# Attention with a threshold and a gated convolution block: 28 of 128 full softmax tiles are transposed by the DMA crossbar, by way of DRAM

## The chip, the cores and the metric

The kernel runs on one core of one Trainium2 chip. The metric is the device time of one execution in microseconds (us). Three runs of the kernel before gave 926.75, 927.73 and 929.31 us; their median is 927.73 us.

## The reference

There are 8 batches of 8 heads, 576 tokens, 64 values to a head. All arrays are float32.

```python
scores = (1/8) * q @ k.T                              # per batch and head, 576 x 576
scores = where(scores >= max(scores) - tau, scores, -1e9)
attn   = exp(scores - max(scores));  attn /= sum(attn) + 1e-9
x      = attn @ v                                     # heads side by side: 576 x 512 per batch
h      = relu(x @ w_in)                               # 576 x 1024
c[t]   = cw[0]*h[t-1] + cw[1]*h[t] + cw[2]*h[t+1]     # along the tokens, per channel
out    = (h * sigmoid(c)) @ w_out                     # 576 x 512
```

## The kernel before

The tokens of a batch are cut into five row tiles: four of 128 rows and one of 64. Two heads are worked on together as a pair, so a batch has four pairs, numbered p = 0 to 3, and the whole run has 160 units of (batch, pair, tile), 128 of them with 128 rows. A batch is walked in two chunks of tiles, (0, 1) and (2, 3, 4); inside a chunk the pairs follow each other, even pairs with the tiles in rising order and odd pairs in falling order.

A unit computes the scores of 128 rows against all 576 keys of both heads (`ps_s`, lines 537 and 544), takes the row maximum on DVE (L552), the exponential on ACT (L561), the mask and row sum on DVE (L564), and scales the rows, mostly on POOL (L597). The result is the tile `em`, 128 x 1152 (two heads of 576). For the product with v it must stand with the keys on the partitions, so it is turned in nine blocks of 128 x 128. TensorE does that against an identity (`turn` and `turns`, L626), four blocks to a PSUM tile `ps_t`; ACT copies each PSUM tile to the tile `eT` of the pair (`group`, L621). `eT` has 128 partitions, nine blocks of 320 columns each, and the row tiles of a chunk lie side by side in the columns. The ninth blocks of the chunk's row tiles share one PSUM tile (`odd`), and the 64-row tile takes one group of four for both heads.

When an odd pair is done, `attend` multiplies `eT` of two pairs with v (`pa`, L676 and L685); ACT and DVE move `pa` into `x` (L692, L695). `ps_t` and `pa` share two PSUM buffers, and `eT` has two buffers. The gated block works chunk by chunk: `mm1` (`ph`, L713), the taps and the gate on DVE, ACT and POOL, and `mm2` (`po`, L786), whose result ACT copies to `ot` (L793) and SP writes out (L794).

SP issues nearly all DMAs, in one in-order queue: loads of q, k and v, the copies `q<-q`, `ks<-ks` and `ks<-xk` that lay out the two halves of a split operand (`halves`, L477), and the stores.

The order of the instructions on each engine is made ahead of time by `Plan.run`. Each step is recorded with `op(engine, ns, function, w=..., r=..., ahead=...)`: a cost in ns, the pieces that it writes and reads, and how far ahead of its place it may go. The planner plays these through, and whatever is ready with the lowest rank goes next on a free engine. Its pieces can be parts of a tile: `(eT, (off, i, k))` is one group's part of `eT`. Waits between engines are put in afterwards, from the memory that each instruction touches. An engine takes its instructions strictly in the order that the planner wrote, and one that waits holds up all behind it.

Of the kernel before, what the change touches and what calls it, by code (L numbers as in the profile page):

```python
# [10 lines left out]
F32 = mybir.dt.float32  # L11
F32R = mybir.dt.float32r
I64 = mybir.dt.int64
U32 = mybir.dt.uint32
AF = mybir.ActivationFunctionType
ALU = mybir.AluOpType
PSUM = bass.MemoryType.PSUM
# [3 lines left out]
AHEAD = {'s': 6.25, 's4': 7.75, 't': 3.5, 'a': 3.5, 'prep': 4.25, 'w': 2.5, 'load': 7.75}  # L21
# [26 lines left out]
}  # L48

JOINT = 2  # L50

KEEP = {'rows': 2.304, 'cols': 1.613, 'turn': 3.226, 'full': 2.304}

# [192 lines left out]
def tile_tau_attention_gated_ffn(  # L246
# [14 lines left out]
    nc = tc.nc  # L261
    P = 128
    B, NP, _, _, S = qd.shape
# [22 lines left out]
    cpool = ctx.enter_context(tc.tile_pool(name="cpool", bufs=1))  # L286
    wk = ctx.enter_context(tc.tile_pool(name="wk", bufs=2))
    sm = ctx.enter_context(tc.tile_pool(name="sm", bufs=4))
    ps_s = ctx.enter_context(tc.tile_pool(name="ps_s", bufs=2, space=PSUM))
    ps_t = ctx.enter_context(tc.tile_pool(name="ps_t", bufs=2, space=PSUM))  # L290
    ps_w = ctx.enter_context(tc.tile_pool(name="ps_w", bufs=2, space=PSUM))
# [23 lines left out]
    def copy(e, dst, src, scale=1.0):  # L315
        if e == "act":
            nc.scalar.activation(dst, src, AF.Copy, scale=scale)
        elif scale == 1.0:
            engines[e].tensor_copy(dst, src)
        else:  # L320
            engines[e].tensor_scalar(dst, src, scale, None, op0=ALU.mult)
# [5 lines left out]
    def sp(n):  # L327
        return 2.6 * n

    def act(n, psum=False):  # L330
        return n * 0.833 + (58 if psum else 95)

    def dve(n, fixed=65):
        return n * 1.07 + fixed
# [4 lines left out]
    def pool1(n):  # L339
        return n * 0.9 + 225  # L340
# [100 lines left out]
    def plain(b):  # L441
        return b == 0
# [73 lines left out]
    def unit(u, k, q1, q2, o, n):  # L516
# [2 lines left out]

        heads = [[0, 1]] if 2 * n <= P else [[0], [1]]  # L520
        m, rows = len(heads), n * len(heads[0])
        em = plan.buf(wk, "em", 4, [P, 2 * S], F32, f"em_{u}")

        few = plan.buf(sm, "few", 4, [P, 10], F32, f"few_{u}")
        a = AHEAD["s" if 2 * n > P else "s4"]
# [79 lines left out]
            )  # L605
        return em

    def transposes(u, ems, tiles, eT):


        em, n, off = ems[-1]

        def group(i, reads, parts, *evacs, width=4 * P):

            pt = plan.buf(ps_t, "ps_t", 2, [P, 512], F32, f"ps_t_{u}_{i}")
            op(
                "pe", width * 0.852, lambda: parts(pt), w=[(pt, 0)], r=reads + [(ident, 0)], ahead=AHEAD["t"], kind="turn"
            )
            for k, (w, dst, src) in enumerate(evacs):
                op(  # L620
                    "act", act(w, True), lambda dst=dst, src=src: nc.scalar.activation(dst(), src(pt), AF.Copy),  # L621
                    w=[(eT, (off, i, k))], r=[(pt, 0)], ahead=AHEAD["t"]
                )

        def turn(pt, at, em, b):
            nc.tensor.transpose(out=pt[:, at:at + P], in_=em[:, int(b * P):int(b * P) + P], identity=ident[:])  # L626

        def turns(pt, b0):
            for i in range(4):
                turn(pt, i * P, em, b0 + i)  # L630

        def both():
            x = eT[:, 0:4, off:off + n]
            return bass.AP(tensor=x.tensor, offset=x.offset, ap=[x.ap[0], [5 * x.ap[1][0], 2], *x.ap[1:]])

        if n < P:
            group(0, [(em, 0)], lambda pt: turns(pt, 0), (4 * P, both, lambda pt: pt[:].rearrange("p (i j n) -> p j i n", i=4, j=2)))
        else:  # L640
            for b0 in (0, 4):
                group(
                    b0, [(em, 0), (em, 1)] if b0 else [(em, 0)], lambda pt, b0=b0: turns(pt, b0),
                    (4 * P, lambda b0=b0: eT[:, b0:b0 + 4, off:off + P], lambda pt: pt[:].rearrange("p (a b) -> p a b", a=4))
                )
        if len(ems) < tiles:
            return
        full, small = ([x for x in ems if (x[1] < P) == y] for y in (False, True))
        w = len(full) * P


        def odd(pt):
            for x in full + small:
                turn(pt, x[2], x[0], 8 if x[1] == P else 3.5)

        parts = [(w, lambda: eT[:, 8, :w], lambda pt: pt[:, :w])]
        for _, m, at in small:
            for j in range(2):
                parts.append((
                    m, lambda j=j: eT[j * D:(j + 1) * D, 4, at:at + m], lambda pt, j=j: pt[D:, w + j * m:w + (j + 1) * m]  # L660
                ))
        group(8, [(x[0], 1 if x[1] == P else 0) for x in full + small], odd, *parts, width=w + len(small) * P)
# [155 lines left out]
    def order(i):  # L818
        c, p = pairs[i]
        return chunks[c].tiles[::-1] if p % 2 else chunks[c].tiles  # L820
# [36 lines left out]
    for now in range(len(units) + 1):  # L857
        plan.rank = float(now)
        if now < len(units):
            i, t = units[now]  # L860
            c, p = pairs[i]
            tiles, (o, w), (a0, an) = order(i), chunks[c].new, chunks[c].cols
            at, n = TILES[t]
            em = unit(now, *(whole[i] if n == P or i not in last else last[i]), at - o if n == P or i not in last else 0, n)
            if t == tiles[0]:
                eT = plan.buf(wk, "eT", 2, [P, NBLK, 320], F32, f"eT_{i}")
                ems = []
            ems.append((em, n, at - o))
            transposes(now, ems, len(tiles), eT)
            if t == tiles[-1]:  # L870
                x = plan.buf(wk, f"x{c % 2}", NP, [P, 2, XW[c % 2]], F32R, f"x_{i}")
                xs.setdefault(c, []).append(x)
                off = o - a0
                if off:
                    y, end = xs[c - 1][p], chunks[c - 1].cols[1]
                    op(
                        "pool", 110, lambda x=x, y=y, off=off, end=end: nc.gpsimd.tensor_copy(x[:, :, :off], y[:, :, end - off:end]),
                        w=[(x, 2)], r=[(y, 0), (y, 1)]
                    )
                waiting.append((i, p, eT, vts[i], x, off))  # L880
# [74 lines left out]
```

## Time and profile before

| | |
|---|---|
| median of three runs | 927.73 us |
| span of the profiled execution | 923.8 us |
| PE matmul busy | 896.7 us, 97% |
| DVE busy | 741.1 us, 80% |
| ACT busy | 701.2 us, 76% |
| POOL busy | 582.1 us, 63% |
| DMA queue of SP and ACT, share of the 16 DMA engines | 38.6% |
| granted TensorE clock | 0.996 |

The span runs from the first to the last instruction of the one execution that was profiled; the times of the runs hold some 4 us beside it. Busy times are sums over the span; since matmuls are pipelined and their ends are modelled, a busy PE need not be one at its peak. In the rows of the profile "x28" is the number of instructions, "<-" stands between what is written and what is read, and the time after a second "<-" is how long the engine sat idle until the named one released it. SPq is SP's issuing of DMAs.

### The profile page before, as it was taken

How to read it: one execution, taken by the hardware profiler on the slowest of the kernel's cores; microseconds unless marked ns; L12 is line 12 of the kernel's file. 1: busy time of each engine (PE TensorE's matmuls, PEld its weight loads, DVE VectorE, ACT ScalarE, POOL GpSimd, SP SyncE). 2: the span in 40 equal slices, each digit the busy share in tenths (PEclk: the TensorE clock that was granted, in tenths of full speed). 3: DMA queues.
4: the chain of work that ended last, by engine and by line, in shares of the span. 5: the costliest groups of instructions: out<-in, count | busy, mean ns of one | idle time of the engine just before them, and what ended most of it. 6: DMA issues, size and time to landing. Idle time of an engine off the chain costs nothing.

```text
span 923.8 us, 19667 instructions
## 1 busy us (share of the span) xinstructions
PE 896.7 (97%) x6308; PEld 731.8 (79%) x6308; DVE 741.1 (80%) x1853; ACT 701.2 (76%) x1590; POOL 582.1 (63%) x1028
## 2 busy tenths in 40 slices
PE   5989899999999999999999999999999999999998
PEld 2446588878889788879888787887888888887897
DVE  5988999979868798878967789886977879896643
ACT  5888898878678787869768687786958788785653
POOL 3665887767747586666746677675865757664422
PEclk9999999999999999999999999999999999999999
DMA  6643363355341652345423453416523265221000
GB/s 211 200 151 128 97 166 101 111 146 167 87 122 40 176 150 83 84 115 140 122 91 81 133 148 103 120 59 166 161 85 95 55 175 140 83 79 60 13 24 34
DMA packets 77926, 104.02 MB, mean 113 GB/s; under 512 B 18560, under 2 KB 49536, under 8 KB 77824
## 3 DMA queue, kind: packets, MB, share of 16 engines
q1 hardware_dynamic: 76960, 100.86, 38.6%
q10 hardware_dynamic: 864, 1.90, 0.6%
q8 instruction: 51, 0.84, 0.4%
q14 instruction: 51, 0.42, 0.1%
HBM read 58.88 MB, written 9.44 MB: 74 GB/s over the span
## 4 chain that ended last, share of the span: by engine, by line
PE 79%; ACT 9%; DVE 6%; issue 2%; DMA 2%; POOL 1%; SPq 0%; ACTq 0%; POOLq 0%; DVEq 0%
PE po L786 21%; PE ph L713 16%; PE ps_t L626 13%; PE pa L685 12%; PE ps_s L544 11%; PE ps_s L537 4%; ACT eT L621 2%; PE pa L676 2%; DVE em L564 2%; ACT em L561 2%; DVE few L552 1%; DVE t L748 1%; PE pw_stage L394 1%; DMA q<-in_qd_dram 1%; ACT hp L728 1%
## 5 line engine op out<-in xcount | busy, mean ns | idle before, releaser
L597 POOL TENSOR_SCALAR em<-em,few 128x576 f32<-128x576 f32 x285 | 258.3, 914 | 36.9 <-DVE few L588 27.3
L564 DVE SCALAR_TENSOR_TENSOR em<-ps_s,few,em 128x576 f32<-128x576 f32 x288 | 228.1, 812 | 51.0 <-ACT em L561 44.9
L713 PE MATMUL ph<-x,w1h 128*128 128x322 f32 (+1 forms) x1024 | 243.2, 305 | 0.7 <-ACT hp L728 0.7
L552 DVE TENSOR_REDUCE few<-ps_s 128x1 f32<-128x576 f32 x288 | 210.8, 748 | 29.4 <-PE ps_s L537 15.2
L561 ACT ACTIVATE em<-ps_s,few 128x576 f32<-128x576 f32 x288 | 206.7, 743 | 30.9 <-DVE few L552 26.0
L621 ACT ACTIVATE eT<-ps_t 128x512 f32<-128x512 f32 (+2 forms) x416 | 203.3, 512 | 16.9 <-PE ps_t L626 15.2
L626 PE MATMUL ps_t<-ident,em 128*128 128x128 f32 x1312 | 187.7, 276 | 4.6 <-DVE x L695 1.7
L626 PEld LDWEIGHTS ps_t<-ident,em 128*128 128x128 f32 x1312 | 152.3, 141 | 34.2 <-POOL em L597 11.0
L713 PEld LDWEIGHTS ph<-x,w1h 128*128 128x128 f32 x1024 | 174.9, 189 | 3.7 <-issue 1.8
L748 DVE SCALAR_TENSOR_TENSOR t<-hp,cw,t 128x255 f32<-128x255 f32 (+1 forms) x256 | 151.9, 597 | 25.9 <-ACT t L732 18.8
L544 PE MATMUL ps_s<-ks,q 128*128 128x288 f32 x896 | 155.0, 304 | 2.6 <-DVE em L564 1.6
L713 PE MATMUL ph<-x,w1l 128*128 128x322 f32 (+1 forms) x512 | 151.1, 295 | 0.0
L544 PEld LDWEIGHTS ps_s<-ks,q 128*128 128x128 f32 x896 | 129.0, 188 | 13.8 <-issue 4.6
L324 POOL TENSOR_TENSOR gl<-t,gh 128x255 fp32r<-128x255 f32 (+9 forms) x192 | 121.4, 644 | 29.4 <-ACT gh L765 29.2
L685 PE MATMUL pa<-eT,v 128*64 128x320 f32 (+1 forms) x1024 | 133.3, 412 | 0.0
L685 PEld LDWEIGHTS pa<-eT,v 128*64 128x64 f32 x1024 | 70.9, 138 | 59.9 <-issue 16.7
L786 PE MATMUL po<-w2h,gh 128*128 128x512 f32 x288 | 118.1, 410 | 0.0
L786 PE MATMUL po<-w2h,gl 128*128 128x512 f32 x288 | 113.0, 392 | 0.5 <-POOL gl L324 0.5
L786 PE MATMUL po<-w2l,gh 128*128 128x512 f32 x288 | 113.1, 393 | 0.0
L713 PEld LDWEIGHTS ph<-x,w1l 128*128 128x128 f32 x512 | 96.6, 189 | 0.1
L755 DVE SCALAR_TENSOR_TENSOR t<-t,hp 128x321 f32<-128x321 f32 (+1 forms) x128 | 70.8, 554 | 14.3 <-ACT t L757 13.6
L757 ACT ACTIVATE t<-t 128x321 f32<-128x321 f32 (+1 forms) x128 | 56.9, 445 | 24.4 <-DVE t L748 24.1
(69 smaller groups left out, 1019.6 us busy)
## 6 DMA issues: line engine op xcount, KB each, us to landing
q<-q SPq DMA_DIRECT2D x336, 64.0 KB, 2.0
v<-in_vc_dram SPq DMA_DIRECT2D x64, 288.0 KB, 3.3
k<-in_kp_dram SPq DMA_DIRECT2D x35, 320.0 KB, 3.6
out_dram<-ot SPq DMA_DIRECT2D x36, 256.0 KB, 2.0
xk<-in_kt_dram SPq DMA_DIRECT2D x28, 288.0 KB, 3.3
ks<-xk SPq DMA_DIRECT2D x56, 144.0 KB, 2.4
xq<-in_qt_dram SPq DMA_DIRECT2D x56, 128.0 KB, 2.3
stage<-in_w_out_dram SPq DMA_DIRECT2D x8, 512.0 KB, 3.5
```

Source lines behind the costliest of these rows:

```text
L324: engines[e].tensor_tensor(dst, x, y, op=ALU.subtract)
L544: nc.tensor.matmul(ps[:, c, :CH], lhsT=q[:, h, o:o + n], rhs=k[:, h, c * CH:(c + 1) * CH], start=(i == 0), stop=(i == 1))
L552: nc.vector.tensor_reduce(few[:rows, nm], ps[:rows, :, :CH], op=ALU.max, axis=mybir.AxisListType.XY, negate=True)
L561: nc.scalar.activation(view(), ps[:rows, :, :CH], AF.Exp, bias=few[:rows, nm])
L564: nc.vector.scalar_tensor_tensor(view(), ps[:rows, :, :CH], few[:rows, th], view(), op0=ALU.is_ge, op1=ALU.mult, accum_out=few[:rows, total])
L597: engines[e].tensor_scalar(sl, sl, by, to, op0=ALU.mult, op1=ALU.add)
L621: "act", act(w, True), lambda dst=dst, src=src: nc.scalar.activation(dst(), src(pt), AF.Copy),
L626: nc.tensor.transpose(out=pt[:, at:at + P], in_=em[:, int(b * P):int(b * P) + P], identity=ident[:])
L685: nc.tensor.matmul(pa[j * D:(j + 1) * D, :w], lhsT=vt[:, blk, :], rhs=eT[:, blk, :w], start=False, stop=(r == 3))
L713: nc.tensor.matmul(ph[:, :an], lhsT=w1[w][:, cb, fs], rhs=xs[cb][:, h, :an], start=(cb == 0 and i == 0), stop=(cb == NCB - 1 and i == 2))
L748: nc.vector.scalar_tensor_tensor(t[:, :kn], hp[:, k:kn + k], cw[:, 3 * f + k:3 * f + k + 1], t[:, :kn], op0=ALU.mult, op1=ALU.add)
L786: nc.tensor.matmul(po[:], lhsT=x[:, f, at:at + P], rhs=w[:, f, :], start=(f == 0 and i == 0), stop=(f == NFB - 1 and i == 2))
```

## The change

In batches 1 to 7 the first row tile of each even pair in each chunk (tile 0 or tile 2; 7 x 2 x 2 = 28 tiles) no longer goes through TensorE. `cross` takes its place:

- Two copies take the float32 tile `em` apart into its low and high 16 bits, `parts` (two planes of 1152 values of 16 bits). One copy is at home on ACT, the other on POOL, and the planner may swap them.
- One DMA of SP writes `parts` to a DRAM tile `rows`, 256 rows of 1152 values (576 KB).
- One transposing DMA of SP reads `rows` and writes all nine blocks of the tile's columns of `eT`, the low and the high half of each value side by side.

The odd group then holds only the ninth blocks of the tiles that TensorE still turns. `em` gets five buffers in place of four, and the room for DMA descriptors of the POOL queue is cut to 1024 bytes.

```diff
+FAR = 3
+EMS = 5
+    far = ctx.enter_context(tc.tile_pool(name="far", bufs=FAR, space=bass.MemoryType.DRAM))
-        em = plan.buf(wk, "em", 4, [P, 2 * S], F32, f"em_{u}")
+        em = plan.buf(wk, "em", EMS, [P, 2 * S], F32, f"em_{u}")
+    def crossed(i, t):
+        c, p = pairs[i]
+        return not plain(chunks[c].b) and p % 2 == 0 and t == order(i)[0]
+
+    def cross(u, em, eT, off):
+        parts = plan.buf(wk, "parts", 2, [P, 2, 2 * S], U16, f"parts_{u}")
+        rows = plan.buf(far, "rows", FAR, [2 * P, 2 * S], U16, f"rows_{u}")
+        a = AHEAD["s"]
+        for j in range(2):
+            def part(e, j=j):
+                src = em[:].bitcast(U16).rearrange("p (k two) -> p k two", two=2)[:, j]
+                copy(e, parts[:, j], src)
+            choice = {"act": act(2 * S), "pool": pool1(2 * S), "dve": dve(2 * S)}
+            home = ("act", "pool")[j]
+            op(home, choice[home], part, w=[(parts, j)], r=[(em, 0), (em, 1)], ahead=a, port=True,
+               other=[(e, ns) for e, ns in choice.items() if e != home])
+        op("sp", sp(2 * S), lambda: nc.sync.dma_start(rows[:].rearrange("(q two) k -> q two k", two=2), parts[:]),
+           w=[(rows, 0)], r=[(parts, 0), (parts, 1)], ahead=a)
+        op("sp", 2000, lambda: nc.sync.dma_start_transpose(eT[:].bitcast(U16)[:, :, 2 * off:2 * off + 2 * P], rows[:]),
+           w=[(eT, (off, i, 0)) for i in range(NBLK)], r=[(rows, 0)], ahead=a)
...
-        if n < P:
+        if ems[-1][3]:
+            cross(u, em, eT, off)
+        elif n < P:
...
-        full, small = ([x for x in ems if (x[1] < P) == y] for y in (False, True))
+        full, small = ([x for x in ems if (x[1] < P) == y and not x[3]] for y in (False, True))
...
-            ems.append((em, n, at - o))
+            ems.append((em, n, at - o, crossed(i, t)))
...
-    nc = bacc.Bacc("TRN2", target_bir_lowering=False, num_devices=1)
+    nc = bacc.Bacc("TRN2", target_bir_lowering=False, num_devices=1, dynamic_dma_scratch_size=1024)
```

Three queues show what moves, all at the same place: the third pair (p = 2) of the second chunk of batch 3, whose `eT` is `eT_5611` before and `eT_5530` in the change. On ACT, before, the three row tiles of this pair (`em_5413`, `em_5498` and the 64-row tile) are copied out of PSUM one group after the other, and each copy waits for PE alone:

```order
L621 ACTIVATE eT_5611<-ps_t_0_5595 128x4x128 [waits PE_49]
L488 ACTIVATE xk_1_5572<-xk_1_5572 128x576 [waits DMAHW3_49,DMAHW0_49]
L463 ACTIVATE q_5588<-q_5588 128x128 [waits DMAHW1_49]
L621 ACTIVATE eT_5611<-ps_t_4_5622 128x4x128 [waits PE_49]
L621 ACTIVATE eT_5611<-ps_t_0_5630 128x4x128 [waits PE_49]
L489 ACTIVATE ks_1_5650<-xk_1_5572 128x576 [waits Activation_49]
L621 ACTIVATE eT_5611<-ps_t_4_5645 128x4x128 [waits PE_49]
```

In the change the first tile (`em_5360`) is taken apart on ACT, and the second tile's two copies to `eT_5530` follow, with one exponential between them:

```order
L322 ACTIVATE parts_5443<-em_5360 128x1152 [waits DMAHW2_49,Pool_49]
L832 ACTIVATE ot_5459<-po_5293 128x512 [waits PE_49]
L566 ACTIVATE em_5480<-ps_s_0_5445,few_5470 128x576 [waits DVE_49]
L566 ACTIVATE em_5486<-ps_s_0_5463,few_5478 128x576 [waits DVE_49]
L731 ACTIVATE x_5182<-pa_5452 128x320 [waits PE_49]
L493 ACTIVATE xk_0_5461<-xk_0_5461 128x576 [waits DMAHW0_49]
L494 ACTIVATE ks_0_5507<-xk_0_5461 128x576 [waits Activation_49]
L731 ACTIVATE x_5189<-pa_5455 128x320 [waits PE_49]
L655 ACTIVATE eT_5530<-ps_t_0_5516 128x4x128 [waits DMAHW2_49,PE_49]
L566 ACTIVATE em_5551<-ps_s_0_5522,few_5538 128x576 [waits DVE_49]
L655 ACTIVATE eT_5530<-ps_t_4_5540 128x4x128 [waits DMAHW4_49,PE_49]
```

The two copies of the first tile are gone, and the last row has a new wait, DMAHW4: the count that it asks for there is the one that the transposing DMA into the same `eT_5530` raises on landing. The two write different columns of that tile, whose memory ranges, from first to last byte, overlap. (The DMAHW2 of the third row from the end is the transposing DMA of the tile that held this buffer earlier.)

On SP in the change, at the same place, the store of the two planes and the transposing DMA stand among the loads of v and the copies for the next batch:

```order
L634 DMA rows_5476<-parts_5443 128x2304 [waits DMAHW1_49,Activation_49,Pool_49]
L833 DMA out_dram<-ot_5459 128x512 [waits DMAHW2_49,Activation_49]
L518 DMA v_5527<-in_vc_dram 128x576 [waits DMAHW3_49,PE_49]
L638 DMA_TRANSPOSE eT_5530<-rows_5476 128x9x256 [waits DMAHW4_49,DMAHW1_49,Activation_49]
L518 DMA v_5576<-in_vc_dram 128x576 [waits DMAHW5_49,PE_49]
L482 DMA ks_0_5507<-ks_0_5507 64x576 [waits DMAHW6_49]
L482 DMA ks_0_5507<-xk_0_5461 64x576 [waits DMAHW7_49,Pool_49]
L482 DMA q_32_5429<-q_32_5429 64x256 [waits DMAHW0_49]
```

The transposing DMA is new here, and it waits for three things: the landing of `rows`, the landing of an earlier DMA that used its semaphore, and an ACT instruction. The ACT count that it asks for is that of the copy `eT_5530<-ps_t_0_5516`, the ninth row of the ACT list.

On PE in the change the stretch from the second tile's second group to the next instruction that needs a `ps_t` buffer back reads:

```order
L660 MATMUL ps_t_4_5540<-ident,em_5422 128x128 [waits DVE_49,Pool_49]
L660 MATMUL ps_t_4_5540<-ident,em_5422 128x128 x3
L660 MATMUL ps_t_0_5546<-ident,em_5480 128x128 [waits Activation_49,Pool_49]
L660 MATMUL ps_t_0_5546<-ident,em_5480 128x128 x3
L825 MATMUL po_5555<-w2h,gh 128x512
L825 MATMUL po_5555<-w2h,gl 128x512
L825 MATMUL po_5555<-w2l,gh 128x512
L825 MATMUL po_5555<-w2h,gh 128x512
L825 MATMUL po_5555<-w2h,gl 128x512
L825 MATMUL po_5555<-w2l,gh 128x512
L660 MATMUL ps_t_8_5567<-ident,em_5422 128x128 [waits Activation_49]
L660 MATMUL ps_t_8_5567<-ident,em_5480 128x128
```

Before these rows stand the second tile's first group (`ps_t_0_5516`, four transposes) and eight matmuls of `ps_s`. The ninth blocks are two here (the second tile's and the small tile's), where before they were three; `ps_t_8_5567` takes the buffer that the waiting ACT copy reads.

More of the change, by code (lines that the diff above doesn't have):

```diff
@@ L14 @@
 U32 = mybir.dt.uint32
+U16 = mybir.dt.uint16
 AF = mybir.ActivationFunctionType
@@ L606, in unit @@
         return em
+    def crossed(i, t):
[7 more added lines that the diff above has]
+            def part(e, j=j):
+                src = em[:].bitcast(U16).rearrange("p (k two) -> p two k", two=2)[:, j]
+                copy(e, parts[:, j], src)
+            choice = {"act": act(2 * S), "pool": pool1(2 * S), "dve": dve(2 * S)}
+            home = ("act", "pool")[j]
+            op(
+                home, choice[home], part, w=[(parts, j)], r=[(em, 0), (em, 1)], ahead=a, port=True,
+                other=[(e, ns) for e, ns in choice.items() if e != home]
+            )
+        op(
+            "sp", sp(2 * S), lambda: nc.sync.dma_start(rows[:].rearrange("(q two) k -> q two k", two=2), parts[:]),
+            w=[(rows, 0)], r=[(parts, 0), (parts, 1)], ahead=a
+        )
+        op(
+            "sp", 2000, lambda: nc.sync.dma_start_transpose(eT[:].bitcast(U16)[:, :, 2 * off:2 * off + 2 * P], rows[:]),
+            w=[(eT, (off, i, 0)) for i in range(NBLK)], r=[(rows, 0)], ahead=a
+        )
     def transposes(u, ems, tiles, eT):
-        em, n, off = ems[-1]
+        em, n, off = ems[-1][:3]
         def group(i, reads, parts, *evacs, width=4 * P):
@@ L647, in transposes @@
             return
-        full, small = ([x for x in ems if (x[1] < P) == y] for y in (False, True))
+        full, small = ([x for x in ems if (x[1] < P) == y and not x[3]] for y in (False, True))
         w = len(full) * P
+        at0 = min((x[2] for x in full), default=0)
         def odd(pt):
[L653 to L657, printed above, removed]
+            for k, x in enumerate(sorted(full + small, key=lambda x: x[2])):
+                turn(pt, k * P, x[0], 8 if x[1] == P else 3.5)
+        if not full + small:
+            return
+        parts = [(w, lambda: eT[:, 8, at0:at0 + w], lambda pt: pt[:, :w])] if full else []
+        for _, m, at, _ in small:
             for j in range(2):
```

## The prediction

> **What bounds the kernel now.** The page comes first: the busy times and the shares of the chain that ended last.
>
> ```profile
> span 923.8 us, 19667 instructions
> PE 896.7 (97%) x6308; PEld 731.8 (79%) x6308; DVE 741.1 (80%) x1853; ACT 701.2 (76%) x1590; POOL 582.1 (63%) x1028
> PE 79%; ACT 9%; DVE 6%; issue 2%; DMA 2%; POOL 1%; SPq 0%; ACTq 0%; POOLq 0%; DVEq 0%
> ```
>
> PE is busy for 97% of the span and carries 79% of the chain. The view by windows and the waits of PE, both for the stretch from 120 to 810 us in which batches 1 to 7 run, say how full it is there.
>
> ```profile
> 120.00:810.00 690.00, 685.87 (x4984) 578.18 (x4986) 573.86 (x1463) 539.78 (x1236) 463.08 (x815) 1.00 0.42 116
> PE ps_t L626 <- ACT eT L621: 0.2, 1, 0.2
> ```
>
> The columns after the length are PE, its weight loads, DVE, ACT, POOL, the granted clock and the DMA share. PE is idle for 4.1 of 690 us, and for copies out of PSUM it waits once, for 0.2 us. So every microsecond of work taken from PE can shorten the run, and nearly every new wait of PE lengthens it. DVE (83% of the stretch) and ACT (78%) have room, but not enough to make good long pauses at once.
>
> **What PE loses.** The chain of waits, drawn from 400 to 460 us, gives the cadence of each kind of matmul on a full PE.
>
> ```profile
> 417.01 0.70 PE po L786 x3
> 417.71 0.87 PE ps_t L626 x8
> 421.68 1.05 PE ps_s L544 x8
> 438.15 0.71 PE ph L713 x6
> 436.65 0.97 PE ph L713 x6
> ```
>
> A transpose costs 0.87 / 8 = 0.109 us; a `po` 0.233, a `ps_s` 0.131, a `ph` 0.118 (narrow chunk) to 0.16. (The mean of 276 ns that the groups show for a transpose is its latency.) The change takes 9 transposes from each of 28 tiles: 252 x 0.109 = **27.4 us less on PE**.
>
> **What the other engines gain and lose.**
>
> ```profile
> L621 ACT ACTIVATE eT<-ps_t 128x512 f32<-128x512 f32 x288 | 166.2, 602 | 14.2 <-PE ps_t L626 13.3
> L488 ACT ACTIVATE xk<-xk 128x576 f32<-128x576 f32 x28 | 19.3, 689 | 2.3 <-DMA xk<-in_kt_dram 2.3
> L503 ACT ACTIVATE q<-xq 128x256 fp32r<-128x256 f32 x56 | 23.2, 414 | 9.7 <-PE ps_s L544 9.7
> L597 POOL TENSOR_SCALAR em<-em,few 128x576 f32<-128x576 f32 x285 | 258.3, 914 | 36.9 <-DVE few L588 27.3
> L324 POOL TENSOR_TENSOR xk<-xk,ks 128x576 fp32r<-128x576 f32 x28 | 40.8, 1458 | 18.2 <-ACT ks L489 11.3 <-PE ps_s L544 5.5 <-DMA v<-in_vc_dram 1.4
> ```
>
> ACT drops two copies of 0.602 us per tile and takes one of 1152 columns. From 256 to 576 columns its copies grow by (689 - 414) / 320 = 0.86 ns a column, so this one is 0.689 + 576 x 0.00086 = 1.18 us: nothing gained or lost. POOL's copy of 1152 values is not in the trace. Two rows of 576 bound it: twice 0.914 = 1.8 us (one operand, as here) to twice 1.458 = 2.9 us. I take 1.8: 28 x 1.8 = 50 us on an engine that idles for 227 of the 690 us. It costs nothing by itself.
>
> **What the new path needs.** Neither the store of 576 KB nor the transposing DMA is in the trace. The nearest DMAs, by their time from issue to landing:
>
> ```profile
> out_dram<-ot SPq DMA_DIRECT2D x36, 256.0 KB, 2.0
> stage<-in_w_out_dram SPq DMA_DIRECT2D x8, 512.0 KB, 3.5
> stage<-in_w_in_dram SPq DMA_DIRECT2D x5, 512.0 KB, 4.3
> stage<-in_w_in_dram ACTq DMA_DIRECT2D x3, 512.0 KB, 8.6
> ```
>
> The store lies between 2.0 us (a store of less than half the size) and 3.9 (the 3.5 row times 576 / 512); I take 3.5. The landing time of the transposing DMA, T, is the one number that decides. Lower end 3.5 us: a plain load of a little less. Upper end 8.6 x 576 / 512 = 9.7 us, the slowest large load. I take **T = 4.8 us**, the 4.3 us row times 576 / 512: the nearest in size and queue, and the slower of the two SP rows because here the data arrives in finer pieces.
>
> The Trainium skill, page "Advanced Engine Details and Errata", section "X-Bar Transpose (TRN2)", says that transposing DMAs are as fast as regular ones, 350 to 400 GB/s. For 590 kB that is an estimate of 1.5 to 1.7 us, and with the fixed 2.0 us that the page "DMA: Bandwidth & Descriptors", section "Anatomy of one DMA — SWDGE (gpsimd) path", gives for another queue, T = 3.5 to 3.7; the sum below would then end near -10 us and not at +8. No run here shows it yet.
>
> **Where it is waited for.** The product with v is far off. This is the timeline of the pair whose queues stand in the section on the change, before, and then the chain:
>
> ```profile
> 402.92 1.63 POOL L597 TENSOR_SCALAR em<-em,few 128x576 f32<-128x576 f32 x2 [0.30 <-DVE few L558]
> 415.44 0.59 ACT L621 ACTIVATE eT<-ps_t 128x512 f32<-128x512 f32 x1
> 416.69 1.08 ACT L621 ACTIVATE eT<-ps_t 128x512 f32<-128x512 f32 x2
> ...
> 439.38 0.70 PE pa L676 x8
> ```
>
> The first tile is normalised at 404.55, its own copies come at 415.44 and 416.69, the second tile's first copy at about 417.2, and `pa` starts at 439.38. The new path needs 1.8 + 3.5 + 4.8 = 10.1 us and its places in the queues; `pa` never waits for it.
>
> The second tile's copies on ACT do. The order of the change shows the knot: on SP the transposing DMA waits for the second tile's first copy, which precedes it in the program; on ACT the second tile's next copy waits for the landing of that DMA, one exponential later. So ACT stops for almost all of T, however early the planes were ready, and everything behind it on ACT stops too: exponentials, `ph` and `po` copies. I went through all 28 tiles in the order. **11 are knotted like this**; in 7 more a copy stands behind the DMA without the DMA waiting for a copy of that tile; in the other 10 no copy of the same tile waits for it.
>
> For the knotted ones: from the end of PE's group that feeds the first copy, ACT needs 0.60 us for that copy, T for the landing, 0.60 for the second copy, and hand-offs of some 0.1:
>
> ```profile
> 402.53 0.60 ACT L793 ACTIVATE ot<-po 128x512 f32<-128x512 f32 x1 [0.90 <-PE po L786]
> 403.15 0.35 SPq L794 DMA_DIRECT2D out_dram<-ot  x1
> ```
>
> (the copy ends at 403.13 and SP issues at 403.15). PE meanwhile has what stands before the next row that needs a PSUM buffer back. At the place shown that is 8 `ps_s`, 8 transposes and 6 `po`: 8 x 0.131 + 8 x 0.109 + 6 x 0.233 = 3.3 us. It loses 4.8 + 1.3 - 3.3 = 2.8 us. Counted in the same way, the eleven covers are 2.1, five times 3.3, 3.4, 3.4, 4.4, 4.9 and 7.3. Ten of them are below 6.1 and sum to 34.7: 10 x 6.1 - 34.7 = **26.3 us lost**; the eleventh loses nothing.
>
> For the seven: if the DMA lands before ACT arrives, 0; if it is issued only when PE ends the feeding group, T + 0.7 less covers of 1.0, 1.1, 1.1, 2.0, 2.2, 5.1, 5.1, together 21 us. By the timeline the second tile's copy came 12.6 us after the first tile's normalisation against the 10.1 that the path needs, so I take 6, nearer to nothing.
>
> SP's own queue: behind the transposing DMA stand a load of v and copies for the next batch, and it holds them until `rows` has landed. At a batch's start the chain runs over such a copy:
>
> ```profile
> 426.56 2.32 DMA q<-q
> ```
>
> Bounds: 0 (PE is standing at the knot anyway) to 7 starts x 3.5 = 25 us. I take 3, since these waits run beside the knots. The fifth `em` buffer and the smaller descriptor room cost nothing: the DMA issues of the page are SP's and ACT's.
>
> **Sum**: -27.4 + 26.3 + 6 + 3 = +7.9 us on the span of 923.8, 931.7. The median of the runs lies 3.9 us above that span; with it, **935.6 us**.
>
> **The rivals.**
>
> *A fast crossbar.* T = 3.5: the knots cost 10 x 4.8 - 34.7 = 13.3, the seven 2, SP 2; -27.4 + 17.3 = -10.1, **917.6 us**. For it: the 3.5 us row, eight times. Against it: that row is a plain load of 512 KB into long runs. The sum, some 14 us per microsecond of T, changes sign at T = 4.2.
>
> *The waits are hidden.* If ACT's queue gets to the knot only when the DMA is down, PE's 27.4 us remain whole: **900.3 us**. Against it: the DMA's issue hangs on the copy only one to three ACT instructions ahead, so nothing but a T of about 2 would do; the shortest large transfer of the trace is 2.0 at 256 KB.
>
> *A slow crossbar.* T = 9.7: the knots cost 11 x 11.0 - 42.0 = 79, the seven some 20, SP 8; +80, **1007 us**. For it: many small pieces, shared with transfers that fill 42% of the DMA time; the trace has a large load at 8.6. Against it: that one ran among the colliding loads of the start.
>
> **How the numbers follow.** Forecast 0.53 (T of 4.1 to 6.5), fast crossbar 0.24, waits hidden 0.05, slow crossbar 0.18. The likeliest case alone spans 926 (T = 4.1) to 960 (T = 6.5). The range 912 to 985 leaves out the hidden waits, the fastest end of the fast crossbar and the upper half of the slow one. 0.3% (2.8 us) is about what a measurement of this kernel can tell from no change; T near 4.2 falls within it, 0.04 of the forecast and 0.04 of the fast crossbar. Faster 0.20 + 0.05 = 0.25, same 0.08, slower 0.49 + 0.18 = 0.67.
>
> **What would show it.** In the profile after: 252 transposes fewer at PE's line 660 and some 27 us less of them. The DMA issues give T outright. ACT's copies to `eT` (L655) should wait for a DMA, about 11 long waits of near 4 us, and PE should show new idle time before `ps_t`, `po` or `ph`, released by ACT, of some 26 us or more. `pa` should wait for no transposing DMA. If T is as taken and ACT's copies show no such waits, the knot is misread; if T is far from 4.8, the size is wrong and the mechanism may stand.

## The result, and the profile after

| | before | after |
|---|---|---|
| median of four runs each, on one chip | 927.24 us (924.38 to 929.31) | 999.78 us (997.03 to 1002.24) |
| span of the profiled execution | 923.8 us | 998.6 us |
| granted TensorE clock | 0.996 | 0.969 |

The changed kernel takes 1.078 times as long as the kernel before (95% interval 1.074 to 1.082): 72.5 us more, where the prediction had 7.9 us more and a range up to 985. The direction was right, the size was not. (A run's time is 1.8 us above its own span, 1000.35 against 998.6 in the profiled one, and not some 4 us as said above; the rest of that difference lies between executions. In the diff above, the view of the two copies reads `p two k`; the letters there are in the wrong order.)

The page of the changed kernel, its busy times and its chain:

```profile
span 998.6 us, 19157 instructions
PE 902.7 (90%) x6056; PEld 724.5 (73%) x6056; DVE 758.0 (76%) x1872; ACT 700.6 (70%) x1544; POOL 618.1 (62%) x1055
PEclk9999899899999999989999999999999998989999
PE 59%; DMA 13%; DVE 9%; ACT 9%; POOL 4%; issue 4%; SPq 1%; ACTq 0%; POOLq 0%; DVEq 0%
```

TensorE does 252 matmuls fewer (x6308 before), yet shows 6 us more of busy time, since in several slices (the 8s of the third line, which gives the granted clock in tenths) its clock is down. Its share of the chain falls from 79% to 59%, and DMA has 13% where it had 2%. The rows of the new operations, from the groups, the DMA issues, and the view of the line that issues the transposing DMA (first its time on SP's queue in ns, least, median and most; then its time from issue to landing):

```profile
L322 ACT ACTIVATE parts<-em 128x1152 uint16<-128x1152 uint16 x28 | 32.6, 1165 | 2.4 <-POOL em L602 2.0 <-POOL hp L762 0.3
L324 POOL COPY parts<-em 128x1152 uint16<-128x1152 uint16 x28 | 33.3, 1189 | 0.3
L660 PE MATMUL ps_t<-ident,em 128*128 128x128 f32 x1060 | 160.0, 282 | 49.2 <-ACT eT L655 43.2 <-POOL em L602 4.0 <-DVE x L734 1.7
```

```profile
rows<-parts SPq DMA_DIRECT2D x28, 576.0 KB, 3.4
```

```profile
L638 SPq DMA_TRANSPOSE eT<-rows x28: 2402/2665/4045, 135.9 to 922.5; - x28
DMA to landing us min/median/max: 4.5/5.0/6.1
```

T is 5.0 us (4.8 was taken), the store 3.4 (3.5), the ACT copy 1.165 us (1.18), the POOL copy 1.19 us (1.8). So no price of the new path explains the miss. The waits do, from the views of all waits and of PE's:

```profile
ACT eT L655 <- DMA eT<-rows: 64.5, 18, 5.6
PE ps_t L660 <- ACT eT L655: 43.2, 17, 5.8
PE po L825 <- ACT hp L767: 10.7, 5, 4.8
```

ACT waits 18 times for a transposing DMA, 64.5 us in all, in the eleven knotted pairs and in the seven others in which a copy stands behind the DMA. TensorE waits for ACT in turn; before, it waited 1.5 us in the whole trace for these copies, and 0.2 us between 120 and 810 us. All idle times of TensorE over 0.3 us, summed over the trace, are 21.0 us before and 89.4 us after: 35.0 of them at the eleven knots, 16.2 at the seven (the pause at each place or the next one behind it), the rest spread.

At the place that the prediction showed (the pair of `eT_5530`) the timeline reads:

```profile
437.50 0.60 ACT L655 ACTIVATE eT<-ps_t 128x512 f32<-128x512 f32 x1
438.13 3.57 SPq L638 DMA_TRANSPOSE eT<-rows  x1
438.83 0.74 ACT L566 ACTIVATE em<-ps_s,few 128x576 f32<-128x576 f32 x1 [0.72 <-DVE few L557]
...
440.41 0.40 PE L825 MATMUL po<-w2l,gh 128*128 128x512 f32 x1
...
443.76 0.60 ACT L655 ACTIVATE eT<-ps_t 128x512 f32<-128x512 f32 x1 [4.19 <-DMA eT<-rows]
444.41 0.69 PE L660 MATMUL ps_t<-ident,em 128*128 128x128 f32 x2 [3.61 <-ACT eT L655]
445.02 0.82 DVE L569 SCALAR_TENSOR_TENSOR em<-ps_s,few,em 128x576 f32<-128x576 f32 x1 [4.53 <-ACT em L566]
...
446.29 0.63 PE L825 MATMUL po<-w2h,gl 128*128 128x512 f32 x1
446.71 0.63 PE L825 MATMUL po<-w2l,gh 128*128 128x512 f32 x1
...
450.29 0.40 PE L825 MATMUL po<-w2h,gh 128*128 128x512 f32 x1
450.53 0.39 PE L825 MATMUL po<-w2h,gl 128*128 128x512 f32 x1
```

This is the knot as predicted: the second tile's first copy ends at 438.10, SP issues the transposing DMA at 438.13, ACT does one exponential and then waits until 443.76, and TensorE stands still for 3.61 us. What the prediction did not have follows: the next `po` matmuls come 0.42 us apart (446.29, 446.71), and only after 450 again 0.24 (450.29, 450.53). The windows of this stretch, and the whole of batches 1 to 7, show why (the column before the DMA share is the granted clock):

```profile
120.00:870.00 750.00, 687.29 (x4735) 567.03 (x4733) 583.52 (x1464) 539.17 (x1193) 489.02 (x826) 0.97 0.56 148
429.00:436.00 7.00, 6.96 (x60) 3.86 (x60) 6.49 (x19) 5.66 (x9) 6.06 (x12) 1.00 0.64 207
436.00:443.00 7.00, 4.80 (x34) 3.57 (x30) 2.92 (x6) 2.54 (x5) 3.13 (x4) 1.00 0.76 145
443.00:450.00 7.00, 5.59 (x18) 4.92 (x19) 3.49 (x9) 4.35 (x10) 2.56 (x4) 0.51 0.65 182
450.00:457.00 7.00, 7.00 (x52) 6.48 (x51) 1.90 (x6) 4.39 (x10) 2.52 (x4) 1.00 0.26 75
```

For the 7 us behind the pause the clock is 0.51. Over the whole span the trace has 3 stretches at half clock before, 9.8 us together, and 14 after, 62.6 us; each is 3.4 or 6.8 us long but for the one cut off at the end. Of the 18 places at which ACT waits, 12 have a TensorE pause of 2.5 us or more; at 10 of these 12 a stretch at half clock begins inside the pause or within 1.2 us of its end. Only two stretches of batches 1 to 7 have no such pause at them; both follow a pause of 1.84 us.

All 14 stretches begin on one grid of 3.413 us. Counted by the windows of this grid from 107 us on, each of the 12 windows at full clock in which TensorE was busy for 46% of the time or less was followed by half clock, and none of those with 48% or more. Two pauses of 2.95 us (at 622.7) and 3.07 us (at 591.4) lay across the edge between two windows, and no stretch followed them. The Trainium skill, page "TensorE: Matmul & The Clock Gate", section "Part 1: The HAM clock gate (the 'warmup' mystery)", says that the array's clock drops to half after an idle window of about 3.4 us and comes back after a busy one. The length of the stretches agrees; that the window must be idle does not: pauses of 2.5 us (at 214.3) and 2.8 us (at 682.5) were followed by a stretch.

### The profile page after: what moved, and what is told of

It reads as the page before. It is cut to its first block, busy times and chain, and to the rows that moved or that the text cites. A ratio compares the mean times of both kernels' runs of the same rounds, so it can differ in the third digit from the quotient of the medians.

```text
span 998.6 us, 19157 instructions
## 1 busy us (share of the span) xinstructions
PE 902.7 (90%) x6056; PEld 724.5 (73%) x6056; DVE 758.0 (76%) x1872; ACT 700.6 (70%) x1544; POOL 618.1 (62%) x1055
## 4 chain that ended last, share of the span: by engine, by line
PE 59%; DMA 13%; DVE 9%; ACT 9%; POOL 4%; issue 4%; SPq 1%; ACTq 0%; POOLq 0%; DVEq 0%
PE po L825 16%; PE ph L752 11%; PE pa L724 10%; PE ps_s L549 9%; DMA eT<-rows 8%; PE ps_t L660 8%; DVE em L569 3%; ACT eT L655 3%; PE ps_s L542 3%; DVE few L557 2%; POOL em L602 2%; ACT em L566 2%; PE pa L715 2%; DVE t L787 2%; DMA q<-q 1%
## 5 line engine op out<-in xcount | busy, mean ns | idle before, releaser
L602 POOL TENSOR_SCALAR em<-em,few 128x576 f32<-128x576 f32 x286 | 261.9, 924 | 39.7 <-DVE few L593 25.1
L655 ACT ACTIVATE eT<-ps_t 128x512 f32<-128x512 f32 (+2 forms) x360 | 168.5, 487 | 105.0 <-DMA eT<-rows 64.5
L660 PE MATMUL ps_t<-ident,em 128*128 128x128 f32 x1060 | 160.0, 282 | 49.2 <-ACT eT L655 43.2
L752 PEld LDWEIGHTS ph<-x,w1h 128*128 128x128 f32 x1024 | 179.6, 195 | 9.1 <-ACT hp L767 3.7
L787 DVE SCALAR_TENSOR_TENSOR t<-hp,cw,t 128x255 f32<-128x255 f32 (+1 forms) x256 | 161.9, 642 | 30.8 <-ACT t L771 23.8
L660 PEld LDWEIGHTS ps_t<-ident,em 128*128 128x128 f32 x1060 | 125.9, 143 | 77.8 <-ACT eT L655 32.1
L549 PE MATMUL ps_s<-ks,q 128*128 128x288 f32 x896 | 163.5, 315 | 13.4 <-DVE em L569 6.5
L549 PEld LDWEIGHTS ps_s<-ks,q 128*128 128x128 f32 x896 | 136.8, 199 | 34.4 <-issue 15.2
L825 PE MATMUL po<-w2h,gh 128*128 128x512 f32 x288 | 122.0, 424 | 10.7 <-ACT hp L767 10.7
L563 POOL TENSOR_SCALAR few<-few,ntau 128x1 f32<-128x1 f32 x99 | 34.9, 354 | 67.2 <-DVE few L557 51.5
```

Source lines behind the costliest of these rows:

```text
L549: nc.tensor.matmul(ps[:, c, :CH], lhsT=q[:, h, o:o + n], rhs=k[:, h, c * CH:(c + 1) * CH], start=(i == 0), stop=(i == 1))
L602: engines[e].tensor_scalar(sl, sl, by, to, op0=ALU.mult, op1=ALU.add)
L752: nc.tensor.matmul(ph[:, :an], lhsT=w1[w][:, cb, fs], rhs=xs[cb][:, h, :an], start=(cb == 0 and i == 0), stop=(cb == NCB - 1 and i == 2))
L787: nc.vector.scalar_tensor_tensor(t[:, :kn], hp[:, k:kn + k], cw[:, 3 * f + k:3 * f + k + 1], t[:, :kn], op0=ALU.mult, op1=ALU.add)
L825: nc.tensor.matmul(po[:], lhsT=x[:, f, at:at + P], rhs=w[:, f, :], start=(f == 0 and i == 0), stop=(f == NFB - 1 and i == 2))
```

## The experiments

Two theories stood at first. **The waits**: ACT's stops behind the transposing DMA, placed there because the memory of the DMA and of the copies overlaps from first to last byte, cost the run its time, directly and through the clock. **The traffic**: the DMAs, the copies and SP's longer queue cost it, wherever anybody waits.

**The transposing DMA last.** Nothing is left out; the DMA is only recorded after all copies into the same `eT`, so that no copy stands behind it.

```diff
+        def land():
             op(
                 "sp", 2000, lambda: nc.sync.dma_start_transpose(eT[:].bitcast(U16)[:, :, 2 * off:2 * off + 2 * P], rows[:]),
-                w=[(eT, (off, i, 0)) for i in range(NBLK)], r=[(rows, 0)], ahead=a
+                w=[(eT, (off, i, 0)) for i in range(NBLK)], r=[(rows, 0)] + [x for x in plan.wrote if x[0] is eT], ahead=a
             )
+        landing.append(land)
...
             transposes(now, ems, len(tiles), eT)
+            while t == tiles[-1] and landing:
+                landing.pop()()
```

> The transposing DMA is recorded after all copies of ACT into the same eT, so that it waits for them and none of them waits for it; copies, store, transposing DMA and the tiles that take the new path stay. Theory 1 (the knot on ACT costs the time, and half of it by way of the clock): ACT waits for no transposing DMA, the granted clock is back at 0.99 or more, PE has some 27 us less work than before: 898 to 915 us. Theory 2 (SP's queue, the DMA traffic or the two copies cost it): all of them are as they were, so the time stays at 960 to 1000 us.

916.67 us, ratio 0.990 (0.987 to 0.993). Page and window of this kernel, and its copies to `eT`:

```profile
span 914.5 us, 19192 instructions
PE 878.5 (96%) x6056; PEld 709.8 (78%) x6056; DVE 759.0 (83%) x1855; ACT 696.6 (76%) x1544; POOL 624.6 (68%) x1072
120.00:810.00 690.00, 679.18 (x4853) 565.85 (x4851) 598.19 (x1483) 545.76 (x1215) 502.62 (x856) 1.00 0.60 162
L660 ACT ACTIVATE eT<-ps_t 128x512 f32<-128x512 f32 x232 | 136.0, 601 | 33.3 <-PE ps_t L665 32.1
```

With the same copies, stores and transposing DMAs, and with more DMA traffic per microsecond (a share of 0.60 against 0.56), the copies wait for PE alone, the clock is 1.00, and TensorE's pauses are 30.1 us. Moving the place of one DMA is worth 83 us, though the time is 1.7 us above the range of the first theory. The waits are the cause; the traffic is not. (The planner's order changes here in other places too; the runs with the columns laid apart, with half of the waits and with the planner told take the waits away by other edits.)

**The path beside the old one.** TensorE turns all tiles as before, `em` has four buffers, and the new path runs in addition, its DMA into a tile `idle` that nobody reads.

```diff
-EMS = 5
+EMS = 4
+        idle = plan.buf(wk, "idle", 1, [P, NBLK, 2 * P], U16, f"idle_{u}")
+        op("sp", 2000, lambda: nc.sync.dma_start_transpose(idle[:], rows[:]), w=[(idle, 0)], r=[(rows, 0)], ahead=a)
-        elif n < P:
+        if n < P:
```

> TensorE turns all tiles as before, and the 28 tiles take the new path as well, into a tile of their own that nobody reads (four em buffers): extra work only, no knot. Theory 1: ACT has some 33 us and POOL some 50 us more work beside a full PE, DMA 33 MB more: 925 to 945 us. Theory 2: the price of queue, traffic and copies shows in full: 975 us or more.

942.27 us, ratio 1.018 (1.014 to 1.021), clock 0.996. The path's work alone costs 17 us (942.27 against 925.33) where TensorE has no relief, and it does not touch the clock.

**The columns laid apart.** `eT` becomes five pieces of 64 columns, so that the memory of different row tiles does not overlap; each of the 28 tiles takes two transposing DMAs of 288 KB.

```diff
-                eT = plan.buf(wk, "eT", 2, [P, NBLK, 320], F32, f"eT_{i}")
+                eT = plan.buf(wk, "eT", 2, [P, 5, NBLK, D], F32, f"eT_{i}")
...
+        for j in range(2):
+            op(
+                "sp", 1500, lambda j=j: nc.sync.dma_start_transpose(
+                    eT[:].bitcast(U16)[:, off // D + j], rows[j * P:(j + 1) * P, :]
+                ),
```

> eT is laid out in five pieces of 64 columns, nine blocks each, so that the memory ranges of the row tiles don't overlap; the tile arrives in two transposing DMAs of 288 KB, one for each 64 columns, and nothing else of the same eT waits for them or makes them wait. Theory 1, with the overlap of memory ranges as its cause: no wait of ACT for a transposing DMA of the same eT, clock at 0.99 or more, 898 to 915 us, and if e1 is slower than this one the wait of the DMA for the copies costs that much. Theory 2: 960 to 1000 us, or more with twice the transposing DMAs.

927.44 us, ratio 1.002 (1.0005 to 1.004), clock 0.994, no copy of ACT waiting for a DMA. From the view of the issuing line and of PE's waits:

```profile
L639 SPq DMA_TRANSPOSE eT<-rows x56: 1257/1494/2381, 134.5 to 850.1; - x56
DMA to landing us min/median/max: 3.7/4.3/6.0
```

```profile
PE ps_t L663 <- POOL em L602: 11.1, 11, 2.0
```

Here the waits go without any DMA being moved behind the copies: so it was the overlap of the ranges that placed them. Expected were 898 to 915 us. That this kernel is 11 us behind the first experiment, which also has no such waits, is not settled; it has twice the DMAs, and the planner put other things in another order (TensorE now waits 11.1 us for scaled rows from POOL).

**The relief alone.** The new path is left out, and the 28 tiles' columns of `eT` are filled with zeros by one POOL instruction each. The product with v still runs, on zeros, so the rows of the 28 tiles are missing from the result.

```diff
+            "pool", pool1(2 * S), lambda: nc.gpsimd.memset(eT[:, :, off:off + P], 0.0),
```

> The new path is left out: the columns of the 28 tiles in eT are filled with zeros by one POOL instruction each, so their rows' products with v are left out of the result. What is measured is PE's relief alone. By the cadence of the chain (252 transposes at 0.109 us) 27 us less: 900 us, give or take 5. If ACT, DVE or the chain at the batches' starts hold the run, the relief is worth less: 912 us or more.

908.69 us, ratio 0.982 (0.978 to 0.985), span 907.4. The page of this kernel:

```profile
PE 874.9 (96%) x6056; PEld 709.7 (78%) x6056; DVE 749.5 (83%) x1858; ACT 671.9 (74%) x1523; POOL 614.3 (68%) x1062
```

TensorE's busy time falls by 21.8 us and the span by 16.4. Without the 252 transposes the run is some 17 us shorter, not 27.4. The path costs 8 us on top (916.67 in the first experiment), half of what it costs without the relief. This run keeps the fifth `em` buffer, which costs 7.8 us when it comes alone (below); the relief with four buffers was not measured.

**Half of the waits.** The DMA goes last in the second chunks only; the first chunks keep the change's order.

```diff
+        if chunks[pairs[units[u][0]][0]].tiles[0]:
+            landing.append(land)
+        else:
+            land()
```

> Only the 14 tiles of the second chunks come last, as in e1; the other 14 are as in the change. In its order ACT still waits for a transposing DMA of the same eT in 11 places (18 in the change, none in e1). If each such wait has the same price, (999.8 - 916.7) / 18 = 4.6 us, it gives 916.7 + 11 x 4.6 = 967 us, with 11 waits of ACT and 6 to 8 stretches of half clock. If it is the whole order of the change and not these waits that cost the time, it lies off that line, near 917 or near 1000.

944.85 us, ratio 1.020 (1.017 to 1.024), clock 0.984. Expected were 967: too many. From the view of the waits:

```profile
ACT eT L663 <- DMA eT<-rows: 19.3, 9, 3.9
PE ps_t L668 <- ACT eT L663: 14.1, 11, 3.9
```

Fewer of the waits that the order still holds were waits on the chip than I had counted; the others found the DMA landed. Against the first experiment, 19.3 us of ACT's waiting cost 28.2 us (1.46 us each), and in the change 64.5 us cost 83.1 (1.29 each). The time goes with the waiting, and a microsecond of it costs more than one.

**The planner told.** Its pieces get the overlap that the memory has, and the DMA's measured price; nothing else.

```diff
-            "sp", 2000, lambda: nc.sync.dma_start_transpose(eT[:].bitcast(U16)[:, :, 2 * off:2 * off + 2 * P], rows[:]),
-            w=[(eT, (off, i, 0)) for i in range(NBLK)], r=[(rows, 0)], ahead=a
+            "sp", 2700, lambda: nc.sync.dma_start_transpose(eT[:].bitcast(U16)[:, :, 2 * off:2 * off + 2 * P], rows[:]),
+            w=[(eT, (off, i, 0)) for i in range(NBLK)] + [(eT, "all")], r=[(rows, 0)], ahead=a, late=300.0
-                    w=[(eT, (off, i, k))], r=[(pt, 0)], ahead=AHEAD["t"]
+                    w=[(eT, (off, i, k)), (eT, "all")], r=[(pt, 0)], ahead=AHEAD["t"]
```

> The waits stay, but the planner knows of them: all parts of one eT are one piece to it, and the transposing DMA is put down with what it took (2.7 us of SP, landing 5.0 us after the issue). In its order ACT waits for the DMA of the same eT at all 28 tiles. Theory 1 in its narrow form (what costs is that the wait comes unplanned, with other work of ACT queued behind): the copies come when the DMA has landed, few PE gaps, clock at 0.99, 905 to 930 us. In its wide form (a wait of ACT for this DMA costs wherever it is): 28 x 4.6 us, 1040 us.

926.15 us, ratio 0.9985 (0.997 to 1.000). The waits are all still in the program, but the planner puts other work before them, and no copy to `eT` stops for a DMA any more. It hurts to wait at the head of an in-order queue, not to have the wait.

**The DMA's price alone.** The first experiment, with the DMA's measured time on SP and to landing in the planner's costs.

```diff
-                "sp", 2000, lambda: nc.sync.dma_start_transpose(eT[:].bitcast(U16)[:, :, 2 * off:2 * off + 2 * P], rows[:]),
+                "sp", 2700, lambda: nc.sync.dma_start_transpose(eT[:].bitcast(U16)[:, :, 2 * off:2 * off + 2 * P], rows[:]),
...
+                late=300.0
```

> e1 with the planner's cost of the transposing DMA as measured (2.7 us of SP, landing 5.0 us after the issue, in place of 2.0 and 4.0). If SP's queue, which it holds for 28 x 2.7 = 75 us, is behind the 8 us between e1 and the relief alone, 908 to 914 us; if not, 915 to 920.

917.68 us, ratio 0.991 (0.9875 to 0.995): no difference. That the planner under-prices SP's queue is not where the path's 8 us go; where they do go stays open.

**Twice as many tiles.** The first experiment with 56 tiles, one in each pair.

```diff
-        return not plain(chunks[c].b) and p % 2 == 0 and t == order(i)[0]
+        return not plain(chunks[c].b) and t == order(i)[p % 2 if chunks[c].tiles[0] else 0]
```

> e1 with twice the tiles: one full tile of every pair, even and odd, in batches 1 to 7 (56). If the relief of PE goes on at the rate of e1 (8.6 us for 28), 905 to 911 us; if the copies, SP (56 x 2.7 us) and the traffic outgrow it, 920 us or more.

961.19 us, ratio 1.0375 (1.033 to 1.042), clock 0.983. From PE's waits:

```profile
PE ph L757 <- ACT hp L772: 13.4, 8, 2.5
PE pa L720 <- DMA eT<-rows: 6.9, 4, 5.5
```

Now the product itself waits for the DMA, up to 5.5 us, and the pauses (68.7 us) bring the half clock back. TensorE's relief has no more to give here.

**The fifth buffer alone.** The kernel before, with five `em` buffers and the smaller room for descriptors.

```diff
-        em = plan.buf(wk, "em", 4, [P, 2 * S], F32, f"em_{u}")
+        em = plan.buf(wk, "em", 5, [P, 2 * S], F32, f"em_{u}")
...
-    nc = bacc.Bacc("TRN2", target_bir_lowering=False, num_devices=1)
+    nc = bacc.Bacc("TRN2", target_bir_lowering=False, num_devices=1, dynamic_dma_scratch_size=1024)
```

> The kernel before with the fifth em buffer and the smaller descriptor room alone. I costed both at nothing: 924 to 930 us. If softmax running one tile further ahead is worth something, part of the relief is due to it: 922 us or less.

934.0 us, ratio 1.0085 (1.007 to 1.010): 7.8 us slower, where the prediction had nothing. The buffer lets the planner make another order, which is the likely reason; this run does not part it from the descriptor room.

**The DMA last, four buffers.** The first experiment with `EMS = 4`.

> e1 with four em buffers in place of five. em is held longer in the 28 tiles, until both copies have read it. If four suffice: 914 to 920 us as e1; if the fifth is what keeps POOL and DVE ahead: 925 us or more.

914.74 us, ratio 0.988 (0.985 to 0.991). It beats both kernels, by 1.2% the one before. Against the first experiment (0.990) the intervals overlap: the 7.8 us are not seen there (the smaller descriptor room stays).

**Half as many tiles.** The first experiment, with the 14 tiles of the second chunks only (`and chunks[c].tiles[0]` in `crossed`).

> e1 with the 14 tiles of the second chunks alone. Half of the relief and half of the DMAs and copies: 921 us, between e1 and the kernel before, if both go by the tile. Nearer to e1 if the second chunks' tiles are the good ones.

921.58 us, ratio 0.995 (0.993 to 0.997): half the tiles, half the gain.

**TensorE kept busy.** The change, with 24 useless transposes behind the second tile's second group in the 13 pairs with a pause of 2.3 us or more. It does more than the change and leaves nothing out.

```diff
+    def fill():
+        for _ in range(24):
+            nc.tensor.transpose(out=spare[0][:, 1, 288:288 + P], in_=ident[:], identity=ident[:])
...
+            if b0 and fills and units[u][0] in FILLED:
+                fill()
```

> The change, with 24 useless transposes of the identity (24 x 0.109 = 2.6 us of TensorE at full clock) into unused PSUM columns, placed right behind the second tile's second group of those 13 pairs in whose wait TensorE stood still for 2.3 us or more (together 45 us). The order on all engines is otherwise that of the change. TensorE gets 34 us of work more. Theory (the granted clock is halved because TensorE stands still, and the halved clock costs the run some 24 us): the fillers run inside the waits, which were there anyway, so they cost about nothing; the pauses shrink to 3 us at most, most half-clock stretches go, and the run becomes shorter though it has more to do: 972 to 988 us, with a mean clock of 0.985 or more in place of 0.969 and TensorE's idle time down by some 33 us. Rival 1 (the slow stretches cost nothing, since ACT's backlog and not TensorE sets the pace behind a wait): the clock rises, but the time stays at 996 to 1004 us. Rival 2 (the clock falls because of the transposing DMAs' traffic or for another reason than the pauses): the clock stays near 0.97, and the time is 1000 us or more, up to 1034.

996.61 us, ratio 1.0756 (1.0725 to 1.0787); span 997.3, clock 0.981. The time that was expected, 972 to 988, was missed, and so was the clock of 0.985; 996.61 lies where rival 1 put it. Its windows at the place shown above:

```profile
436.00:443.00 7.00, 6.53 (x50) 5.72 (x49) 2.86 (x6) 3.04 (x7) 2.47 (x3) 1.00 0.78 199
443.00:450.00 7.00, 7.00 (x44) 5.99 (x43) 4.51 (x13) 4.73 (x13) 4.42 (x7) 1.00 0.44 122
```

The pause is filled and the clock stays up: 44 matmuls against 18 in the same window (18 of `po` against 8). Over the run TensorE's pauses fall from 89.4 to 62.2 us and the half clock from 62.6 to 40.1 us, with the same 28 transposing DMAs and ACT waiting for them nearly as long (61.5 us against 64.5). So it is the pauses that bring the clock down, and rival 2 falls.

What the clock costs is less plain. Of the 34 us of fillers only 27 lay in pauses, which leaves 7 us of plain cost, and TensorE's other matmuls were busy for 8 us less (928.7 less 34, against 902.7). The two cancel, so the time of the whole run does not tell this reading from rival 1, by which neither costs anything. I cut both runs at the 28 transposing DMAs and compared the 27 pieces: beyond what fillers and pauses explain, a piece got shorter by 0.26 us for each microsecond of half clock that it lost (correlation 0.75). Without allowing for fillers and pauses it is 0.34 us, with a standard error of 0.10, where rival 1 would have nothing. Work at half speed would give up to 0.5. By these slopes the clock's share of the 74.8 us is an estimate of 14 to 26 us, for 52.8 us more of half clock; it is argued and not shown, since a run that moves the clock alone was not tried.

## Why the prediction missed

By the terms of its sum on the span, +7.9 predicted and +74.8 measured:

| term | predicted | in the runs |
|---|---|---|
| 252 transposes fewer | -27.4 | -17 (the relief alone) |
| eleven knots | +26.3 | +35.0 of TensorE's pauses |
| seven copies behind the DMA | +6 | +16.2 |
| SP's queue | +3 | +3.6 (TensorE's waits for `q<-q`) |
| other new pauses | 0 | +14 |
| half clock | no term | +14 to +26 (estimate) |

These terms sum to 65 to 77. The step that failed is the price of the waits, 26.3 + 6 + 3 = 35.3 us: each was priced once, as the time in which TensorE stands still at that place, with all that follows at full speed. The first experiment shows what they cost: with the same work and without the waits the run is 83.1 us shorter. In its trace TensorE's pauses are 59.3 us less (30.1 against 89.4), and the same 6056 matmuls are busy for 24.2 us less (878.5 against 902.7), with 13.7 us of half clock in place of 62.6. So the sum lacked pauses away from the knots, and it had no term for the **half clock** behind a pause. The granted clock of 0.996 before is that of a kernel whose TensorE never stops for long, and I took it as given. How much of the 24.2 us the run would have got back at full clock stays open.

The **knots** were right in place, in number and in form: eleven pairs, and T + 1.3 less the cover, with the T of each place, gives 28.6 us of the 35.0 measured there (at the pair shown, 5.55 + 1.3 - 3.3 = 3.55 against 3.61). What it lacks is that a late ACT meets the next waits late too: at one pair ACT waited 4.2 us where the formula has no pause, and TensorE stopped for 2.6 us further on.

The **seven** were mis-sized. I took 6 of at most 21 us because, in the timeline before, the second tile's copy came 12.6 us after the first tile's scaling and the path needed 10.1. On the chip ACT waited at all seven, up to 5.6 us. From the store's issue to the DMA's landing I had taken 3.5 + 4.8 = 8.3 us; at the seven it took 9.3 to 15.0. The two DMAs together took 7.8 to 8.7 us at four of them and 9.4 to 10.7 at three, and between the store's landing and the DMA's issue lay 0.02 to 6.4 us in which SP did other things or waited for something else. I had named "its places in the queues" and given them no time. The 14 us of **other pauses** are spread over the run; in the timeline DVE stands still for 4.53 us behind the same stop, so such stops may be their cause, which is not shown. **SP's queue** was about right: TensorE now waits for the copies `q<-q`, for which it did not wait before.

```profile
PE ps_s L549 <- DMA q<-q: 3.6, 5, 1.4
```

The **relief** was over-sized: a transpose's cadence of 0.109 us was right (TensorE's busy time in this group fell by 27.7 us), but in the run with the relief alone the span fell by only 16.4: TensorE's idle time rose from 27.1 to 32.5 us, and its whole busy time fell by 21.8 and not 27.4, which I could not place. **T** and the price of ACT's copy were right; POOL's copy, at 1.19 us, lay below the lower bound that was given for it. That **`pa` never waits** for the path was right with 28 tiles; with 56 it did. That the **fifth buffer costs nothing** was wrong by itself (7.8 us) and open within the change.

Of the rivals none had the mechanism. The slow crossbar gave 1007 us, near the measured time, but by T = 9.7, which the DMA rows refute. The estimate of T = 3.5 to 3.7 that the prediction worked out from the Trainium skill, page "Advanced Engine Details and Errata", section "X-Bar Transpose (TRN2)", with a fixed 2.0 us added, does not agree with the trace, whose least landing is 4.5 and whose median is 5.0.

## What to carry to other kernels

Where waits are put in by memory range, as here, a transfer that writes part of a tile which other engines are still filling makes them wait if the ranges overlap, though no byte is shared. Issue it after their writes, or lay the parts apart, and tell the planner of it otherwise. On a TensorE that is 97% busy, price a pause that takes about half of a 3.4 us window by its length plus, as an estimate from this case, a quarter to a half of the 3.4 or 6.8 us that run at half clock behind it. And measure what a relief is worth by leaving the work out altogether, before building the path that replaces it: here that bound was 2%.

## What the hardware showed unexpectedly

- Issuing the transposing DMA of 576 KB holds SP's queue for 2.4 to 4.0 us (median 2.67), one of 288 KB for 1.49, a plain store of the same 576 KB for 0.36:

```profile
L634 SPq DMA_DIRECT2D rows<-parts x28: 344/358/536, 129.9 to 914.3; - x28
```

- A transposing DMA of 288 KB lands after 4.3 us (median), one of 576 KB after 5.0: most of T does not go with the size.
- Half clock came after pauses as short as 1.84 us in the change and 1.67 us in the run with fillers, and not after some of 2.95 and 3.07 us. What told was the share of a window of the 3.413 us grid: in the 14 traces together, from 107 us on, 38 of the 39 windows at full clock with TensorE busy for 46% or less were followed by half clock, and 2 of the 3304 others, both at 52%.
- ACT and POOL take 1.17 and 1.19 us for the same 16-bit copy of 1152 values with a stride of two, while POOL's scaling of 576 float32 values takes 0.924.
